# Spectra of neighbouring blocks: combined on VectorE, or accumulated in PSUM

## The chip, the cores and the metric

The kernel runs on one core of one Trainium2 chip. The metric is the device time of one execution in microseconds, the median of several runs. Every run that is quoted here was in the fast state, and each experiment was timed against the kernel before, in the same rounds and on the same chip. The experiments ran in four sets, each on a chip of its own, so a comparison of two of them from different sets is good to some tenths of a us only (the median of the kernel before was 357.57 to 358.05 us in these sets). A verdict of faster or slower needs 2%, which is 7.2 us here; what is discussed below is mostly smaller than that, so the intervals matter more than the verdicts.

## The reference

Two layers, each an H3-style block (a 4-tap shift convolution on `k`, a product with `v`, a long causal convolution by FFT, a product with `q`) and a SwiGLU feed-forward block. `k`, `v` and all weights are the same in both layers.

```python
def _A_ref(q, k, v, shift_k, ssm_k, ssm_D):          # S = 2048, D = 512, 4 taps
    k_shift = 0
    for t in range(ks):
        k_shift = k_shift + k_pad[:, t:t + S, :] * shift_k[:, ks - 1 - t]
    kv = k_shift * v
    y = irfft(rfft(kv, padded) * rfft(ssm_k, padded))[:S]    # causal convolution per channel
    y = y + kv * ssm_D
    return q * y

def _B_ref(x, w_gate, w_up, w_down):                  # F = 1792
    return (silu(x @ w_gate) * (x @ w_up)) @ w_down

for _ in range(2):
    x = x + _A_ref(layernorm(x), A_k, A_v, A_shift_k, A_ssm_k, A_ssm_D)
    x = x + _B_ref(layernorm(x), B_w_gate, B_w_up, B_w_down)
```

All tensors are bf16.

## The kernel before

The long convolution is cut into 4 blocks of 512 rows. A block `b` of the long kernel `h` gets a spectrum `H[b]` by matmuls with cosine and sine tables (`fwd`), copied out of PSUM (the memory that TensorE's matmuls write to; this copy is called evacuation) by ScalarE and finished by additions and subtractions of its parts (butterflies) on VectorE. The spectrum that the products need, `G[b]`, belongs to an overlapped kernel: the h of block `b` together with the h of block `b-1`. Before, `G[b]` is put together on VectorE from two finished spectra:

```python
def by_residue(rows, ev, scale, ring, engs, conv):
    for r in range(R):                                   # R = 4 residues
        for part, f in enumerate(("C", "nS")):           # real, imaginary
            ps = new(ring, "ps", [P, D], F32)
            add("PE", pe(1), ... mm(ps.t[:], [(fT(f, r), rows.t[:, r, :])]) ...)
            evacuate(ps, ev, (2 * r + part,), ..., scale, engs[...], conv)

def fold_h(b):
    h, hp = butterfly4(H[b], True, first if b == 1 else ()), H[b - 1]
    g = G[b] = spectrum(f"G{b}")
    for part, op in ((0, ALU.subtract), (1, ALU.add)):
        dve(4 * D, ... nc.vector.tensor_tensor(out=g.t[:, :, part, :], in0=h.t[:, :, part, :],
                                               in1=hp.t[:, :, 1 - part, :], op=op), ...)
```

`add` does not issue an instruction. It puts an operation with a planned duration into a plan, which a list scheduler orders per engine; `due` dates, the stretch factors and the start times at the top of the file are constants that were found by a search. So any change of an operation or of a constant can reorder all engines, and planned durations (`lat` for a DMA) decide only the order, not the truth.

Three other parts matter below. The h of a block is turned either by TensorE (`transpose_h`) or by a ScalarE copy and DMA transposes on SyncE's queue (`transpose_h_dma`, for the blocks in `H_DMA`):

```python
def transpose_h_dma(b):
    for dt in range(KD):
        add("ACT", ..., nc.scalar.copy(out=hr.t[:, :, dt], in_=hn[b].t[:, dt, :].rearrange(...)))
    for r in range(R):
        turned[b] = add("SP", 1.25, ... nc.sync.dma_start_transpose(out=hs.t[:, r]..., in_=hr.t[:, r]) ...)
```

The shift convolution of a block runs either on TensorE (`shift_mul`: 64 matmuls of 128 columns with diagonal matrices `dg`, which VectorE builds from the taps) or, for the blocks in `K_ACT`, as 16 scaled copies on ScalarE, three sums on VectorE and DMA transposes (`shift_mul_t`). And the taps are loaded as four rows of 1 KB, first on SyncE's queue, and turned by four small TensorE transposes:

```python
tapR = new("dn", "tapR", [KD, P, KS])
add("SP", 0.5, lambda: nc.sync.dma_start(out=tapR.t[:],
    in_=A_shift_k.rearrange("(dt p) j -> dt p j", p=P)), w=[tapR], lat=2.4, due=-70)
...
def turn_taps():
    for j in range(KS):
        nc.tensor.transpose(pt4.t[:, j, :], tapR.t[:, :, j], ident.t[0:KD, 0:KD])
add("DVE", 0.1, lambda: nc.vector.tensor_copy(out=tapT.t[:], in_=pt4.t[:].rearrange("p j dt -> p dt j")), ...)
for dt in range(KD):
    add("DVE", 0.6, ... tensor_tensor(out=dg.t[:, dt], ident (broadcast), tapT.t[:, dt, :] (broadcast), mult))
```

In the names of the profile, `kTb`, `vt` and `hs` are k, v and h of a block in the layout that the next step needs (`hn` and `hr` are h before it is turned), `dg` the diagonal matrices, `G` and `H` the spectra, `z` and `ptz` the normalised rows and their transposes for the feed-forward block, and `pf`, `sg` and `ht` its gate and up products. `wm` are dummy matmuls, which only keep TensorE at work until data are there.

## Time and profile before

| | before |
|---|---|
| median of 2 runs | 357.74 us (357.62 to 357.85) |
| span of the profiled execution (which took 358.32 us) | 356.5 us |
| TensorE (PE) busy | 347.6 us, 97% |
| VectorE (DVE) busy | 281.1 us, 79% |
| ScalarE (ACT) busy | 238.0 us, 67% |
| start of the first spectrum on TensorE | 14.34 us |

The busy line, the slices, the waits and the groups of before are shown in the prediction below. What it does not show is the start, instruction by instruction. In the timeline the columns are the start in us, the duration, the engine, the line and the operation, what it writes and reads, the shape and the number of instructions; in brackets, if any, the idle time before and what ended it.

```profile
5.63 2.50 DVE L933 TENSOR_TENSOR dg<-ident,tapT 128x512 bf16<-128x512 bf16 x4
7.07 1.05 PE L379 MATMUL pt<-ident,kn 128*128 128x128 bf16 x16
8.05 2.44 DVE L385 COPY kTb<-pt 128x512 bf16<-128x512 bf16 x2
10.77 3.74 PE L335 MATMUL ps<-dg,kTb 128*128 128x128 bf16 x64
14.34 3.62 PE L335 MATMUL ps<-hs,fwd 128*128 128x512 bf16 x15
```

VectorE builds the four diagonal matrices first and has finished just as TensorE's first transposes of k come in, so its two copies of k follow at once. The 64 shift matmuls start at 10.77 us and the first spectrum at 14.34.

### The profile page before, as it was taken

To read this page: it belongs to the slowest core of one execution; us is meant where nothing else is said; L and a number is where in the kernel's file an instruction comes from. 1 tells how busy PE (TensorE), PEld (TensorE's weight loads), DVE (VectorE), ACT (ScalarE), POOL (GpSimd) and SP (SyncE) were. 2 spreads that over 40 slices of the span, in tenths; PEclk is the share of its full clock that TensorE was granted. 3 is DMA by queue.
4 is the path that set the end of the run, shared out by engine and by line. 5 is a ranking of instruction groups with operands and counts; after the bars stand their busy time and mean duration, and the time that the engine had idled before them with its cause. 6 is when DMAs were issued, how large, how long until landed. Compare 5 with 4: busy or idle time off the path is not lost.

```text
span 356.5 us, 6735 instructions
## 1 busy us (share of the span) xinstructions
PE 347.6 (97%) x2689; PEld 254.4 (71%) x2712; DVE 281.1 (79%) x517; ACT 238.0 (67%) x454; POOL 39.3 (11%) x42
## 2 busy tenths in 40 slices
PE   7999999999999999999999999999999999999996
PEld 6655985867778585868668685858686777768673
DVE  6997999999989999999999999889985323626020
ACT  4587693838878493648878994848484775647352
POOL 1010010130320200111121000201101000101000
PEclk9999999999999999999999999999999999999999
DMA  7999021010241341010311042010103020101000
GB/s 263 306 353 293 2 69 22 0 31 2 45 119 45 63 147 31 0 31 1 79 40 31 1 116 63 2 29 3 31 29 31 30 31 1 31 1 31 30 2 29
DMA packets 37897, 21.98 MB, mean 62 GB/s; under 512 B 29797, under 2 KB 35690, under 8 KB 37866
## 3 DMA queue, kind: packets, MB, share of 16 engines
q1 hardware_dynamic: 37336, 21.03, 22.9%
q10 hardware_dynamic: 530, 0.53, 0.5%
q8 instruction: 21, 0.34, 0.4%
q14 instruction: 10, 0.08, 0.1%
HBM read 12.33 MB, written 2.10 MB: 40 GB/s over the span
## 4 chain that ended last, share of the span: by engine, by line
PE 49%; DVE 35%; ACT 10%; POOL 3%; issue 2%; DMA 1%; ACTq 0%; POOLq 0%; DVEq 0%
PE pf L335 30%; PE pd L851 15%; DVE m L518 4%; DVE ht L844 3%; DVE bnst L706 3%; DVE t L641 3%; DVE t L635 3%; DVE t L651 2%; POOL rstd L736 2%; ACT H L423 2%; DVE Z L656 2%; PE ps L335 2%; PE wm L1020 1%; DVE t L620 1%; DVE Z L648 1%
## 5 line engine op out<-in xcount | busy, mean ns | idle before, releaser
L335 PE MATMUL pf<-zT,wu_sb 128*128 128x256 bf16 x896 | 116.1, 273 | 0.1
L335 PE MATMUL pf<-zT,wg_sb 128*128 128x256 bf16 x896 | 116.1, 273 | 0.0
L335 PEld LDWEIGHTS <-wg_sb 128*128 128x128 bf16 x896 | 87.6, 98 | 18.9 <-issue 0.8
L851 PE MATMUL pd<-wd_sb,ht 128*128 128x512 bf16 x434 | 98.6, 380 | 1.5 <-DVE ht L844 0.8
L335 PEld LDWEIGHTS <-wu_sb 128*128 128x128 bf16 x896 | 87.6, 98 | 11.1
L837 ACT ACTIVATE sg<-pf 128x512 bf16<-128x512 f32 x112 | 68.9, 615 | 18.2 <-PE pf L335 16.7
L851 PEld LDWEIGHTS <-ht 128*128 128x128 bf16 x448 | 43.6, 98 | 49.8 <-DVE ht L844 1.2
L841 ACT CAST ht<-pf 128x512 bf16<-128x512 f32 x112 | 67.3, 601 | 15.0 <-PE pf L335 14.6
L844 DVE TENSOR_TENSOR ht<-ht,sg 128x1024 bf16<-128x1024 bf16 x64 | 39.5, 619 | 25.7 <-ACT ht L841 25.7
L711 POOL TENSOR_TENSOR rstd<-ve,nhalf 128x2 f32<-128x2 f32 x25 | 26.0, 1039 | 203.2 <-DVE ve L709 180.8
L706 DVE BATCH_NORM_STATS2 bnst<-xc 128x6 f32<-128x512 bf16 x50 | 32.5, 685 | 6.2 <-ACT xc L857 5.6
L863 ACT CAST dn<-pd 128x512 bf16<-128x512 f32 x24 | 12.9, 591 | 34.5 <-PE pd L851 34.5
L870 DVE TENSOR_TENSOR xc<-xc,dn 128x1024 bf16<-128x1024 bf16 x12 | 8.2, 686 | 17.8 <-ACT dn L863 17.8
L635 DVE TENSOR_TENSOR t<-X,G 128x2048 bf16<-128x2048 bf16 x18 | 21.9, 1219 | 0.0
L641 DVE TENSOR_TENSOR t<-X,G 128x2048 bf16<-128x2048 bf16 x18 | 21.9, 1217 | 0.0
L736 POOL TENSOR_TENSOR rstd<-ve,nhalf 128x2 f32<-128x2 f32 x7 | 12.0, 1719 | 80.0 <-DVE ve L732 80.0
L423 ACT ACTIVATE X<-ps 128x512 bf16<-128x512 f32 x32 | 18.8, 635 | 1.2 <-PE ps L335 1.1
L423 ACT ACTIVATE H<-ps 128x512 bf16<-128x512 f32 x24 | 13.4, 645 | 4.3 <-PE ps L335 4.3
L656 DVE TENSOR_TENSOR Z<-Z,t 128x2048 bf16<-128x2048 bf16 x12 | 14.7, 1222 | 0.1
L651 DVE TENSOR_TENSOR t<-t,t 128x2048 bf16<-128x2048 bf16 x12 | 14.6, 1221 | 0.1
L335 PE MATMUL ps<-vt,fwd 128*128 128x512 bf16 x54 | 14.4, 380 | 0.1
L335 PEld LDWEIGHTS <-fwd 128*128 128x128 bf16 x96 | 9.3, 98 | 7.2
(95 smaller groups left out, 316.5 us busy)
## 6 DMA issues: line engine op xcount, KB each, us to landing
vt<-in_A_v_dram SPq DMA_DIRECT2D x4, 512.0 KB, 4.6
xc<-in_A_q_dram SPq DMA_DIRECT2D x4, 512.0 KB, 4.8
out_dram<-xc SPq DMA_DIRECT2D x16, 128.0 KB, 1.7
wg_sb<-in_B_w_gate_dram SPq DMA_DIRECT2D x1, 1792.0 KB, 9.2
wu_sb<-in_B_w_up_dram SPq DMA_DIRECT2D x1, 1792.0 KB
wd_sb<-in_B_w_down_dram SPq DMA_DIRECT2D x1, 1792.0 KB, 12.3
hn<-in_A_ssm_k_dram SPq DMA_DIRECT2D x3, 512.0 KB, 7.6
hn<-in_A_ssm_k_dram ACTq DMA_DIRECT2D x1, 512.0 KB, 3.9
```

What stands on the lines that cost most here:

```text
L335: nc.tensor.matmul(o, lhsT=lhsT, rhs=rhs, start=(n == 0), stop=(n == len(terms) - 1))
L423: add("ACT", act(D), lambda: nc.scalar.activation(out=view(), in_=ps.t[:], func=ACT.Copy, scale=scale), r=[ps], w=[(buf, keys)], conv=conv)
L635: dve(n * D, lambda t1=t1, part=part: nc.vector.tensor_mul(out=t1.t[:], in0=x.t[:, sl, 0, :], in1=g.t[:, sl, part, :]), [(x, key(slots, (0 ...
L641: dve(n * D, lambda t2=t2, part=part: nc.vector.tensor_mul(out=t2.t[:], in0=x.t[:, sl, 1, :], in1=g.t[:, sl, 1 - part, :]), [(x, key(slots ...
L651: dve(n * D, lambda t1=t1, t2=t2, comb=comb: nc.vector.tensor_tensor(out=t1.t[:], in0=t1.t[:], in1=t2.t[:], op=comb), [t2], [t1], conv=conv)
L656: dve(n * D, lambda t1=t1, part=part: nc.vector.tensor_add(out=z.t[:, sl, part, :], in0=z.t[:, sl, part, :], in1=t1.t[:]), [t1], [zk], con ...
L706: add("DVE", 0.6, lambda st=st, i=i: nc.vector.bn_stats(out=st.t[:], in_=xs[c].t[:, i, :]), r=[(xs[c], (i,))], w=[st])
L711: add("POOL", PW, lambda: nc.gpsimd.tensor_tensor(out=rstd.t[:], in0=ve.t[:], in1=nhalf.t[:].to_broadcast((P, n)), op=ALU.pow), r=[ve, nha ...
L837: add("ACT", act(D), lambda ps=ps, o=o, sg=sg: nc.scalar.activation(out=sg.t[:, o:o + 2, :], in_=ps.t[:], func=ACT.Silu), r=[ps], w=[(sg, ...
L841: add("ACT", act(D), lambda ps=ps, o=o, ht=ht: nc.scalar.copy(out=ht.t[:, o:o + 2, :], in_=ps.t[:]), r=[ps], w=[(ht, (o // 2,))], due=(uni ...
L844: dve(n * W, lambda sg=sg, ht=ht: nc.vector.tensor_mul(out=ht.t[:], in0=ht.t[:], in1=sg.t[:]), [sg], [ht], due=(unit, k / pairs, 0.0, "h"))
L851: nc.tensor.matmul(pds[o].t[:], lhsT=ht.t[:, q, o * P:(o + 1) * P], rhs=wt["d"].t[:, ft, :], start=(ft == 0 and not xpe), stop=(ft == NF - 1))
```

## The change

The intent: a spectrum is linear, so `G[b]` can be accumulated in PSUM from the turned h of both blocks, with two matmuls in a tile instead of one. The two-input operations of `fold_h` go, six of 2048 elements in the program. To take TensorE work away in return, and to use VectorE's freed time, the shift convolution of block 2 moves off TensorE (`K_ACT`), and the transposes of block 1's h too (`H_DMA`). All searched constants are new. Two edits stand beside this: the taps are now loaded in their final layout by one DMA on ScalarE's queue, and a gate on the loads for block 2 is gone.

```diff
-H_DMA = lambda b: b in {2, 3}
+H_DMA = lambda b: b in {1, 2, 3}
-K_ACT = lambda b: b in {3}
+K_ACT = lambda b: b in {2, 3}
-RINGS = {}
+G_PE = True
+RINGS = {"hs": 2, "s8": 9} if G_PE else {}
 ... (SLK, ST1, ST2, ASL, HSL, Z_ACT, N_ACT, X_PE, T0, FLOOR, DUR, STRETCH: new values)
-          ("nC", 1, 3), ... ("S", 3, 0)]
+          ("nC", 1, 3), ... ("S", 3, 0), ("S", 0, 0)]
 ... (planned landings of the first loads: h 5.0 to 6.0, k 4.0 to 5.3, v 5.0 to 6.0, x 6.0 to 7.0)
     def spectrum_h(b, ring="pc"):
         hs = transpose_h_dma(b) if H_DMA(b) else transpose_h(b, ring, (0, 2), True)
-        H[b] = forward4(hs, "H", 2.0 / N, ring, True)
+        hss[b] = hs
+        H[b] = spectrum_g(b, ring) if G_PE else forward4(hs, "H", 2.0 / N, ring, True)
+
+    def spectrum_g(b, ring="pc"):
+        hs, hp = hss[b], hss[b - 1]
+        ev = spectrum(f"G{b}")
+        for r in range(R):
+            for part, fs in enumerate((("C", "S"), ("nS", "C"))):
+                ps = new(ring, "ps", [P, D], F32)
+                add("PE", pe(2), ... mm(ps.t[:], [(fT(f, r), t.t[:, r, :]) for f, t in zip(fs, (hs, hp))]), ...)
+                evacuate(ps, ev, (2 * r + part,), ..., 2.0 / N, "ACT", True)
+        return ev
     def fold_h(b):
+        if G_PE:
+            G[b] = butterfly4(H[b], True, first if b == 1 else ())
+            return
 ...
-    tapR = new("dn", "tapR", [KD, P, KS])
-    add("SP", 0.5, lambda: nc.sync.dma_start(out=tapR.t[:], in_=A_shift_k.rearrange("(dt p) j -> dt p j", p=P)), w=[tapR],
-        lat=2.4, due=-70)
+    add("ACT", 0.5, lambda: nc.scalar.dma_start(out=tapT.t[:], in_=A_shift_k.rearrange("(dt p) j -> p dt j", p=P)), w=[tapT],
+        lat=4.2, due=-60)
     load_h(0, "ACT", -59)
 ... (turn_taps and the copy behind it: removed)
         if c + 1 < NB:
-            gate = list(first) if c == 1 else ()
-            load_h(c + 1, after=gate)
-            load_k(c + 1, after=gate)
-            load_v(c + 1, after=gate)
+            load_h(c + 1)
+            load_k(c + 1)
+            load_v(c + 1)
```

More of the change, by code (lines that the diff above doesn't have):

```diff
@@ L19 @@
 NB = 4
-SLK = 8.52
-H_DMA = lambda b: b in {2, 3}
-ST1 = lambda l, c, h: (l, c, h) in {(0, 1, 1), (0, 2, 0), (0, 3, 0), (1, 0, 1)}
-ST2 = lambda l, c, h: (l, c, h) in {(0, 1, 1), (0, 3, 1), (1, 0, 0)}
-ASL = 8.04
-K_ACT = lambda b: b in {3}
+SLK = 10.9
+H_DMA = lambda b: b in {1, 2, 3}
+ST1 = lambda l, c, h: (l, c, h) in {(0, 0, 1), (0, 1, 0), (0, 2, 0)}
+ST2 = lambda l, c, h: (l, c, h) in {(0, 2, 0), (1, 1, 0), (1, 3, 0)}
+ASL = -36.31
+K_ACT = lambda b: b in {2, 3}
 PASSES = 1
@@ L28 @@
 PD_ACT, KV_ACT, ST_ACT = True, True, False
-HSL = 13.4
-Z_ACT = lambda l, c, h: (l, c, h) in {(0, 3, 1), (1, 1, 0), (1, 1, 1)}
-N_ACT = lambda l, c, h: (l, c, h) in {(0, 2, 0), (0, 2, 1), (1, 2, 1), (1, 3, 0), (1, 3, 1)}
+HSL = 21.03
+Z_ACT = lambda l, c, h: (l, c, h) in {(0, 0, 1), (0, 2, 0), (0, 2, 1), (0, 3, 0), (1, 0, 1), (1, 1, 0), (1, 1, 1), (1, 3, 1)}
+N_ACT = lambda l, c, h: (l, c, h) in {(0, 3, 1), (1, 0, 1), (1, 1, 1), (1, 2, 1), (1, 3, 1)}
 Z_DMA = lambda i, j: False
 D_DMA = lambda l, c, h: False
-X_PE = lambda l, c, h: (l, c, h) in {(0, 3, 1), (1, 1, 0), (1, 2, 0), (1, 3, 1)}
-RINGS = {}
-T0, FLOOR = 37.71, 9.21
-DUR = [20.73, 19.38, 17.95, 16.46, 26.14, 17.1, 26.09, 16.75, 22.3, 20.61, 21.16, 19.35, 17.53, 22.2, 16.85, 27.0]
-STRETCH = {1: {"PE": 2.88, "DVE": 1.23, "ACT": 4.33, "POOL": 1.0, "SP": 160.46},
-           2: {"PE": 3.08, "DVE": 1.77, "ACT": 1.75, "POOL": 1.0, "SP": 1.07},
-           3: {"PE": 3.04, "DVE": 1.08, "ACT": 2.72, "POOL": 1.0, "SP": 1.04}}
+X_PE = lambda l, c, h: (l, c, h) in {(0, 2, 0), (0, 2, 1), (0, 3, 1), (1, 0, 1), (1, 3, 1)}
+G_PE = True
+RINGS = {"hs": 2, "s8": 9} if G_PE else {}
+T0, FLOOR = 48.08, 19.94
+DUR = [16.0, 23.9, 26.05, 22.97, 21.86, 19.8, 19.06, 26.96, 19.52, 23.55, 21.07, 24.15, 16.63, 23.57, 17.87, 26.61]
+STRETCH = {1: {"PE": 8.53, "DVE": 2.37, "ACT": 2.97, "POOL": 1.0, "SP": 14.17},
+           2: {"PE": 2.62, "DVE": 1.0, "ACT": 1.41, "POOL": 1.0, "SP": 2.29},
+           3: {"PE": 6.2, "DVE": 1.34, "ACT": 1.62, "POOL": 1.0, "SP": 2.04}}
 R = 4
@@ L47 @@
           ("nS", 0, 2), ("nS", 1, 2), ("nS", 2, 2), ("nS", 3, 2),
-          ("nC", 1, 3), ("nC", 2, 3), ("nC", 3, 3), ("S", 1, 0), ("S", 2, 0), ("S", 3, 0)]
+          ("nC", 1, 3), ("nC", 2, 3), ("nC", 3, 3), ("S", 1, 0), ("S", 2, 0), ("S", 3, 0), ("S", 0, 0)]
 BI = {(f, r): i for i, (f, r, _) in enumerate(BLOCKS)}
@@ L338 @@
     NT = len(BLOCKS)
-    NI = NT // 2
+    NI = 7
     warm1 = whole("warm", [P, 1], F32)
@@ L344 @@
     dg = whole("dg", [P, KD, KS, P], parts=KD)
-    fwd, inv = whole("fwd", [P, NT, P], parts=4), whole("inv", [P, NT, P], parts=2)
+    fwd, inv = whole("fwd", [P, NT, P], parts=5), whole("inv", [P, 2 * NI, P], parts=2)
     wt = {"g": whole("wg_sb", [P, KD, F]), "u": whole("wu_sb", [P, KD, F]), "d": whole("wd_sb", [P, NF, D])}
@@ L358, in load_h @@
         q = nc.sync if eng == "SP" else nc.scalar
-        return add(eng, 0.55, lambda: q.dma_start(out=hn[b].t[:], in_=h3[:, :, b * L:(b + 1) * L]), w=[hn[b]], lat=(5.0, 10.0)[b] if b < 2 else 6.0, due=due, after=after)
+        return add(eng, 0.55, lambda: q.dma_start(out=hn[b].t[:], in_=h3[:, :, b * L:(b + 1) * L]), w=[hn[b]], lat=(6.0, 10.0)[b] if b < 2 else 6.0, due=due, after=after)
     def load_k(b, due=None, after=()):
@@ L363, in load_k @@
             kn[b] = new("s8", "kn", [P, R, D])
-            add("SP", 0.55, lambda: nc.sync.dma_start(out=kn[b].t[:], in_=k_t[:, b]), w=[kn[b]], lat=4.0, due=due)
+            add("SP", 0.55, lambda: nc.sync.dma_start(out=kn[b].t[:], in_=k_t[:, b]), w=[kn[b]], lat=5.3, due=due)
             return
@@ L389, in load_v @@
         vt[b] = new("v", "vt", [P, R, D], parts=R)
-        return add("SP", 0.6, lambda: nc.sync.dma_start(out=vt[b].t[:], in_=v_t[:, b]), w=[vt[b]], lat=4.5 if b else 5.0, due=due, after=after)
+        return add("SP", 0.6, lambda: nc.sync.dma_start(out=vt[b].t[:], in_=v_t[:, b]), w=[vt[b]], lat=4.5 if b else 6.0, due=due, after=after)
     def load_x(c, due=None, after=()):
         xs[c] = new("x", "xc", [P, R, D], parts=R)
-        return add("SP", 0.7, lambda: nc.sync.dma_start(out=xs[c].t[:], in_=q_t[:, c]), w=[xs[c]], lat=4.5 if c else 6.0, due=due, after=after)
+        return add("SP", 0.7, lambda: nc.sync.dma_start(out=xs[c].t[:], in_=q_t[:, c]), w=[xs[c]], lat=4.5 if c else 7.0, due=due, after=after)
     def load_weights(which, due, after=()):
@@ L435, in half @@
                 add("PE", pe(2), lambda ps=ps, terms=terms: mm(ps.t[:], [(fT(f, r), rows.t[:, r, :]) for f, r in terms]),
-                    r=[(rows, [r for _, r in terms]), fwd], w=[ps], conv=conv)
+                    r=[(rows, [r for _, r in terms]), (fwd, range(4))], w=[ps], conv=conv)
                 evacuate(ps, ev, (2 * slot + part,), lambda slot=slot, part=part: ev.t[:, slot, part], scale,
@@ L460, in direct @@
                 add("PE", pe(4), lambda ps=ps, terms=terms: mm(ps.t[:], [(fT(f, r), rows.t[:, r, :]) for f, r in terms]),
-                    r=[rows, fwd], w=[ps])
+                    r=[rows, (fwd, range(4))], w=[ps])
                 evacuate(ps, dst, (2 * slot + part,), lambda slot=slot, part=part: dst.t[:, slot, part], 1.0, engs[part],
@@ L545, in butterfly4 @@
         return ev
+    hss = {}
     def spectrum_h(b, ring="pc"):
         hs = transpose_h_dma(b) if H_DMA(b) else transpose_h(b, ring, (0, 2), True)
-        H[b] = forward4(hs, "H", 2.0 / N, ring, True)
+        hss[b] = hs
[6 more added lines that the diff above has]
+                ps = new(ring, "ps", [P, D], F32)
+                add("PE", pe(2), lambda ps=ps, fs=fs, r=r: mm(ps.t[:], [(fT(f, r), t.t[:, r, :]) for f, t in zip(fs, (hs, hp))]),
+                    r=[(hs, (r,)), (hp, (r,)), fwd], w=[ps], conv=True, dest=ev)
+                evacuate(ps, ev, (2 * r + part,), lambda r=r, part=part: ev.t[:, r, part], 2.0 / N, "ACT", True)
+        return ev
     def fold_h(b):
+        if G_PE:
+            G[b] = butterfly4(H[b], True, first if b == 1 else ())
+            return
         h, hp = butterfly4(H[b], True, first if b == 1 else ()), H[b - 1]
@@ L922 @@
             r=[(fwd, (n,))], w=[(fwd, (part,))])
+    add("DVE", 0.14, lambda: nc.vector.tensor_scalar(out=fwd.t[:, NT - 1, :], in0=fwd.t[:, 4, :], scalar1=-1.0, scalar2=None,
+                                                     op0=ALU.mult), r=[(fwd, (1,))], w=[(fwd, (4,))], due=30.0)
     tapF = whole("tapF", [P, KD, KS], F32)
-    pt4 = new("pf", "pt4", [P, KS, KD], BF16)
-    def turn_taps():
-        for j in range(KS):
-            nc.tensor.transpose(pt4.t[:, j, :], tapR.t[:, :, j], ident.t[0:KD, 0:KD])
-    add("PE", 0.25, turn_taps, r=[tapR, ident], w=[pt4])
-    add("DVE", 0.1, lambda: nc.vector.tensor_copy(out=tapT.t[:], in_=pt4.t[:].rearrange("p j dt -> p dt j")), r=[pt4], w=[tapT])
     add("DVE", 0.1, lambda: nc.vector.tensor_copy(out=tapF.t[:], in_=tapT.t[:]), r=[tapT], w=[tapF])
@@ L939 @@
     add("DVE", 0.34, lambda: nc.vector.tensor_add(out=hs.t[0:1, 0, :], in0=hs.t[0:1, 0, :], in1=drow.t[:]), r=[drow], w=[(hs, (0,))])
+    hss[0] = hs
     shift_mul(0, "pf", False)
@@ L953, in go @@
                 nc.tensor.transpose(it.t[:, i, :], fwd.t[:, n * NI + i, :], ident.t[:])
-        add("PE", pe(NI, P), go, r=[fwd, ident], w=[it])
+        add("PE", pe(NI, P), go, r=[(fwd, range(4)), ident], w=[it])
         add("ACT", act(NI * P), lambda it=it, n=n: nc.scalar.copy(out=inv.t[:, n * NI:(n + 1) * NI, :], in_=it.t[:]),
```

## The prediction

> **What bounds the kernel now.** I read the page first for the busy shares and the forty slices.
>
> ```profile
> PE 347.6 (97%) x2689; PEld 254.4 (71%) x2712; DVE 281.1 (79%) x517; ACT 238.0 (67%) x454; POOL 39.3 (11%) x42
> ...
> PE   7999999999999999999999999999999999999996
> ...
> DVE  6997999999989999999999999889985323626020
> ```
>
> The reader is to see TensorE without a gap between the second and the last slice, and VectorE nearly full for about 30 of the 40 slices but never alone. A busy TensorE need not run at its peak, so I went next to the chain that ended last, in order of time, where nothing but feed-forward matmuls stand after 190 us:
>
> ```profile
> 310.18 6.04 PE pd L851 x28
> 316.22 12.23 PE pf L335 x112
> ```
>
> That is 6.04/28 = 0.216 us for a 512-column matmul and 12.23/112 = 0.109 us for a 256-column one, back to back. For 128 columns the timeline has 64 of them in 3.74 us, of which some 0.16 us is the drain of the last, so about 0.056 us each. With these rates I counted the recorded matmuls of each 20 us window: 20.1 us of matmul work in 40 to 60, 19.6 in 60 to 80, 20.0, 20.2, 20.1 and 20.0 in the next four, 19.6 in 160 to 180, 19.8, 19.8, and 20.0 on average after that. So TensorE is not only busy, it is at its rate from 20 us to the end; the slack in all those windows together is under 2 us. What is left idle or cold is the start (8.4 of the first 20 us) and the end (3.7 us after the last full stretch). Third view, who waited for whom on TensorE:
>
> ```profile
> PE wm L1020 <- POOL ident masks.py:199: 1.7, 1, 1.7
> PE pt L475 <- ACT kTb L383: 1.5, 2, 0.8
> PE pd L851 <- DVE ht L844: 0.8, 2, 0.6
> ```
>
> These are all its named waits. Only the last, 0.8 us, is VectorE's doing. Hence the time is start + TensorE work + under 2 us of stalls + tail. VectorE appears with 35% in the chain of waits because its convolution backlog reaches 190 us, but TensorE fills that time with other units.
>
> **What the Trainium skill says.** "TensorE: Matmul & The Clock Gate", section Back-to-back issue gap, gives N/2.4 + 2.5 ns warm, thus 215.7 and 109.2 ns for 512 and 256 columns: the two chain lines above agree to the last digit. (Its other figure there, 131 ns sustained for 512 columns, does not fit this trace.) "PSUM — Partial Sum Buffer", section The four PSUM rules: a matmul without the first flag adds to what its group has written. So the sum of two neighbouring blocks costs one more matmul and no more evacuations; the 32 X0 spectra of this kernel, four terms each, already work so. "VectorE: DVE Perf Modes", section The perf-mode tier table, has 1224 ns for a bf16 two-input operation of 2048 elements; the trace has 1215 and 1218 for the very instructions that go. The first of these pages, section Part 1: The HAM clock gate, says that the clock is halved until some 3.4 to 4 us of matmuls have run; here the dummy matmuls start 0.107 us apart and speed up only after about 6.2 us.
>
> **The change part by part.** The order of instructions per engine gives exact counts; TensorE first, since it is the bound. The groups touched:
>
> ```profile
> L335 PE MATMUL ps<-dg,kTb 128*128 128x128 bf16 x192 | 11.7, 219 | 0.1
> L335 PE MATMUL ps<-hs,fwd 128*128 128x512 bf16 x39 | 11.7, 379 | 0.2
> ...
> L475 PE MATMUL pt<-ident,hn 128*128 128x128 bf16 x32 | 2.5, 219 | 1.5 <-ACT kTb L383 1.5
> ```
>
> - Two-term spectra of h: 24 evacuated tiles now take two matmuls each (40 to 64 in the program): 24 x 0.216 = +5.2 us.
> - The shift convolution of block 2 goes from TensorE to ScalarE and DMA transposes: 192 to 128, 64 x 0.056 = -3.6 us.
> - The transposes of h for block 1 go to ScalarE and DMA: 32 to 16, 16 x 0.056 = -0.9 us.
> - One more unit adds its residual by an identity matmul (8 to 10): +0.4 us.
> Sum on the bound: **+1.1 us**. The dummy matmuls (46 to 64) are no work but fill the start.
>
> VectorE: the combination goes,
>
> ```profile
> L555 DVE TENSOR_TENSOR G<-H 128x2048 bf16<-128x2048 bf16 x4 | 4.8, 1215 | 0.0
> ...
> L555 DVE TENSOR_TENSOR G<-H,G 128x2048 bf16<-128x2048 bf16 x2 | 2.4, 1218 | 0.0
> ```
>
> -7.2 us. The moved shift adds three 2048-element sums, 3.6 us. Ten normalisations of 0.41 us move to ScalarE, -4.1, with five small scale tiles back, +0.8; two more pairs of row statistics, +1.7; one residual sum less, -0.7. Net about **-6 us**, beside TensorE work: the wait it could remove is the 0.8 us above. ScalarE: 16 scaled copies of k at 0.8 us, ten normalisations at 0.8, four copies of h at 0.7, minus the statistics, four ks and two hs copies: about **+15 us** of 238, also beside.
>
> The start is on the path. The taps now come by one DMA of 8-byte pieces behind the first h, where before four 1 KB rows came first and TensorE turned them. k is issued about 0.46 us earlier, but the rewritten program plans later landings for all first loads and puts 64 dummies in one run. Before, 46 dummies and the taps ended at 7.03 us and k's transposes began at 7.07. 64 from 1.72 us, cold at 0.107 until about 6.2 and then 0.06, end near 7.5 to 7.7: **+0.5 us**.
> Then the first unit's own chain. ScalarE gets four h copies and one statistics pass among the eight X0 evacuations; stepping through its order with the trace's durations, the last evacuation is 2.3 us later and the last Z some 1.6 us later. TensorE has its 16 transposes no longer as filler there, so it idles about **+0.7 us** before the last inverse matmuls. Behind them 14 inverse and 16 spectrum matmuls (6.5 us) cover the 6 us until the normalised rows are back, provided that the DMA transposes of h, queued behind the weights, keep up.
> Elsewhere I take **-1.0 us**, my choice: all tuned constants were searched anew, and a lighter VectorE should close part of the under 2 us of scattered stalls and of the wait for ht. Sum: +1.1 + 0.5 + 0.7 - 1.0 = +1.3, so 357.7 becomes 359.0 us.
>
> **The rivals.** (a) VectorE's relief is worth more than TensorE's extra, so it gets faster by several us. For it: VectorE is mostly at 95% and more until 260 us and holds 35% of the chain. Against: TensorE at its rate in those windows leaves under 2 us to win; even with all of it and nothing lost at the start, 357.7 + 1.1 - 2 = 356.8. (b) ScalarE becomes a local bound. For it: summing durations unit by unit in the new order, one unit of block 1 has 22.2 us of TensorE, 21.7 of VectorE and 20.9 of ScalarE, a later one 21.7, 21.6 and 21.5, so any misfit there is paid; 2 to 3 us, thus 361 to 362. Against: before too had units where VectorE's sum was above TensorE's (22.2 against 20.2), and other units took it up. (c) The start: taps or h transposes land late behind the weight loads (the page shows 353 GB/s in that slice), and VectorE or TensorE waits; 1 to 3 us more, up to 362. (d) The extra matmuls are hidden in idle TensorE: the windows speak against it.
>
> **Range and chances.** The lower end 356.8 is (a) at its fullest; the upper 361.5 is the sum with half of (b) or (c). 2% is 7.2 us, and neither the work counted nor any rival reaches it: faster 0.02, same 0.96, slower 0.02.
>
> **What would show it.** In the changed profile, TensorE's busy share should stay at 97%, the spectrum group should show 64 matmuls and the shift group 128, and the 20 us windows should again hold 19.5 to 20 us of work. VectorE should fall to about 275 us busy and ScalarE rise to about 253. k's transposes should begin at about 7.6 us, and TensorE show a new wait for Z near 30 us. I am wrong if TensorE's windows show more than 2 us of new gaps between 60 and 200 us (then b), if the first feed-forward matmul comes over 3 us later (then c), or if TensorE's gaps before vanish and the start is not later (then a).

## The result and the profile after

The changed kernel takes 362.74 us (median of 2 runs, 362.55 to 362.92) against 357.74, a ratio of 1.014 with a 95% interval of 1.0096 to 1.0183. The changed kernel run again, in other rounds, gave 362.24 and 1.0134 [1.0108, 1.016], with 361.35 to 363.44 in four runs. Ratios here are the mean time of one kernel's fast runs over that of the other's of the same rounds, so not quite the ratio of the medians. The change makes the kernel about 5.0 us slower; that is within 2%, as expected, but above the predicted range, whose upper end was 361.5.

The page of the changed kernel, busy shares and two of the slices:

```profile
PE 350.8 (97%) x2646; PEld 254.5 (70%) x2672; DVE 275.6 (76%) x508; ACT 252.4 (70%) x470; POOL 34.6 (10%) x42
...
PE   7699999999999999999999999999999999999996
...
DVE  3888789999999994699999999999995423525120
```

TensorE is full from the third slice on, as before. Its second slice fell from 9 to 6, VectorE's first from 6 to 3. The loss is at the left edge. TensorE's named waits (in all, how often, the longest):

```profile
PE wm L1033 <- POOL ident masks.py:199: 1.7, 1, 1.7
PE pt L476 <- ACT kTb L384: 1.5, 2, 0.8
PE pt L476 <- DVE kTb L386: 1.1, 1, 1.1
PE ps L336 <- DVE kTb L386: 0.5, 1, 0.5
PE pf L336 <- ACT sg L856: 0.4, 1, 0.4
```

Two of the new ones, 1.6 us, are on VectorE's copies of k. The timeline of the start shows why these are late and what follows:

```profile
1.23 0.52 ACTq L909 DMA_DIRECT2D tapT<-in_A_shift_k_dram  x1
...
7.56 1.05 PE L380 MATMUL pt<-ident,kn 128*128 128x128 bf16 x16
...
8.83 1.90 DVE L946 TENSOR_TENSOR dg<-ident,tapT 128x512 bf16<-128x512 bf16 x3 [3.48 <-DMA tapT<-in_A_shift_k_dram]
...
10.64 2.43 DVE L386 COPY kTb<-pt 128x512 bf16<-128x512 bf16 x2
...
13.13 5.21 PE L336 MATMUL ps<-dg,kTb 128*128 128x128 bf16 x64 [0.55 <-DVE kTb L386]
```

VectorE idles 3.48 us for the taps. Its first copy of k is behind three `dg` operations in its order, so it comes at 10.64 us instead of 8.05, and the shift matmuls start at 13.13 instead of 10.77. Then the same 64 matmuls take 5.21 us instead of 3.74. The windows say why; after the width, the columns are busy time and count of TensorE, weight loads, VectorE, ScalarE and GpSimd, then the granted TensorE clock, the DMA share and GB/s. After:

```profile
7.50:13.13 5.63, 2.43 (x33) 2.00 (x32) 4.30 (x6) 3.46 (x4) 0.00 (x0) 0.98 1.04 396
13.13:18.18 5.05, 5.05 (x64) 5.05 (x64) 4.12 (x9) 1.45 (x4) 0.00 (x0) 0.69 1.13 220
```

Before:

```profile
7.50:13.13 5.63, 4.15 (x71) 3.89 (x69) 5.32 (x10) 3.45 (x4) 0.00 (x0) 1.00 0.95 338
10.77:14.34 3.57, 3.57 (x67) 3.57 (x66) 3.22 (x9) 0.46 (x1) 0.00 (x0) 1.00 1.13 393
```

After a stretch in which TensorE worked 2.43 of 5.63 us, the clock was granted at 0.69 on average while the shift matmuls ran; before, with 4.15 us of work in the same stretch, it stayed at 1.00. The Trainium skill describes this in "TensorE: Matmul & The Clock Gate", section Part 1: The HAM clock gate: half the clock after an idle window of about 3.4 us. The trace agrees on the halved rate (matmuls of this group start 0.107 us apart until about 16 us), though TensorE was never idle for 3.4 us at a stretch here. But from the first dummies to the next matmuls that are no transposes it ran only transposes. This stretch was 5.41 to 6.05 us long in the four profiles in which the clock fell at the start (the changed kernel's two, a_gate and b_newtaps), and 4.42 us at most in the fourteen others, in which it did not. Whether transposes count as work for the clock was not tested.

The first spectrum thus starts at 18.18 us, 3.84 later than before. The chain that ended last, in order of time (start, duration, what), tells the same story:

```profile
1.23 7.50 DMA tapT<-in_A_shift_k_dram
8.83 1.90 DVE dg L946 x3
10.72 2.36 DVE kTb L386 x2
13.13 5.43 PE ps L336 x65
```

From the first spectrum to the end the profiled span has 361.1 - 18.18 = 342.9 us, against 356.5 - 14.34 = 342.2 before. That difference, 0.8 us, is near the +1.1 of counted matmul work (the profiled execution of before was 0.6 us above its median, so the difference may be larger). The groups, with count, busy time and mean ns:

```profile
L336 PE MATMUL ps<-hs,fwd 128*128 128x512 bf16 x58 | 15.9, 379 | 0.3
...
L336 PE MATMUL ps<-dg,kTb 128*128 128x128 bf16 x128 | 9.2, 240 | 0.5 <-DVE kTb L386 0.5
...
L476 PE MATMUL pt<-ident,hn 128*128 128x128 bf16 x16 | 1.4, 218 | 2.6 <-ACT kTb L384 1.5 <-DVE kTb L386 1.1
```

They are as predicted: 128 shift matmuls and 16 transposes of h, and 58 of the 64 spectrum matmuls are recorded. On this reading, the explanation was simple: the new way of loading the taps costs 3.8 us, and the rest behaves. The experiments show that it is not that simple.

### The profile page after: what moved, and what is told of

Same layout as the page of the kernel before. It is cut to its first block, busy times and chain, and to the rows that moved or that the text cites. A ratio compares the mean times of both kernels' runs of the same rounds, so it can differ in the third digit from the quotient of the medians.

```text
span 361.1 us, 6673 instructions
## 1 busy us (share of the span) xinstructions
PE 350.8 (97%) x2646; PEld 254.5 (70%) x2672; DVE 275.6 (76%) x508; ACT 252.4 (70%) x470; POOL 34.6 (10%) x42
## 3 DMA queue, kind: packets, MB, share of 16 engines
q10 hardware_dynamic: 1058, 0.53, 0.5%
## 4 chain that ended last, share of the span: by engine, by line
PE 73%; DVE 11%; ACT 10%; DMA 2%; issue 1%; ACTq 0%; POOL 0%; POOLq 0%; DVEq 0%
PE pf L336 41%; PE pd L870 21%; PE ps L336 9%; DMA tapT<-in_A_shift_k_dram 2%; DVE m L519 2%; PE ps L713 2%; ACT G L424 2%; ACT sg L856 2%; ACT ka L597 1%; DVE ht L863 1%; ACT ht L860 1%; DVE bnst L725 1%; ACT kc L597 1%; DVE X L525 1%; DVE Z L675 1%
## 5 line engine op out<-in xcount | busy, mean ns | idle before, releaser
L730 POOL TENSOR_TENSOR rstd<-ve,nhalf 128x2 f32<-128x2 f32 x26 | 27.3, 1051 | 236.7 <-DVE ve L728 171.3
L725 DVE BATCH_NORM_STATS2 bnst<-xc 128x6 f32<-128x512 bf16 x52 | 33.6, 684 | 4.0 <-ACT xc L876 3.5
L882 ACT CAST dn<-pd 128x512 bf16<-128x512 f32 x22 | 11.8, 592 | 28.8 <-PE pd L870 28.8
L336 PEld LDWEIGHTS <-fwd 128*128 128x128 bf16 x120 | 11.6, 98 | 9.6 <-DMA hs<-hr 0.4
L876 ACT CAST xc<-pd 128x512 bf16<-128x512 f32 x10 | 5.4, 590 | 16.9 <-PE pd L870 16.9
L336 PE MATMUL ps<-hs,fwd 128*128 128x512 bf16 x58 | 15.9, 379 | 0.3
L795 DVE TENSOR_TENSOR n<-n,Yk 128x1024 bf16<-128x1024 bf16 x15 | 10.3, 690 | 6.6 <-ACT Yk L699 5.6
```

What stands on the lines that cost most here:

```text
L336: nc.tensor.matmul(o, lhsT=lhsT, rhs=rhs, start=(n == 0), stop=(n == len(terms) - 1))
L725: add("DVE", 0.6, lambda st=st, i=i: nc.vector.bn_stats(out=st.t[:], in_=xs[c].t[:, i, :]), r=[(xs[c], (i,))], w=[st])
L730: add("POOL", PW, lambda: nc.gpsimd.tensor_tensor(out=rstd.t[:], in0=ve.t[:], in1=nhalf.t[:].to_broadcast((P, n)), op=ALU.pow), r=[ve, nha ...
```

## The experiments

### Is it the taps' load?

**a_oldtaps** is the changed kernel with the old load of the taps.

```diff
-    add("ACT", 0.5, lambda: nc.scalar.dma_start(out=tapT.t[:], in_=A_shift_k.rearrange("(dt p) j -> p dt j", p=P)), ...)
+    tapR = new("dn", "tapR", [KD, P, KS])
+    add("SP", 0.5, lambda: nc.sync.dma_start(out=tapR.t[:], in_=A_shift_k.rearrange("(dt p) j -> dt p j", p=P)), ..., due=-70)
 ... (turn_taps and its copy as before)
```

> The changed kernel with only the load of the taps put back: four rows of 1 KB issued first, turned on TensorE. Theory (the late taps are what the prediction missed): taps are on VectorE by about 5.6 us, the shift matmuls of block 0 start near 11.2 us and the first spectrum matmul near 14.8 us instead of 18.2, so 362.7 - 3.4 = about 359.3 us. Rival (the spectra, the moved shift or the shifted schedule cost it; the taps are hidden): at least 361.5 us.

Measured: 363.22 us, 1.0152 [1.0135, 1.0169]. The theory as stated fell: nothing was won, though the first spectrum now starts at 15.07 us, 3.1 earlier than in the changed kernel. A new wait has swallowed it, the first line of TensorE's waits:

```profile
PE ps L336 <- DMA hs<-hr: 2.7, 1, 2.7
```

The timeline of this kernel shows the wait and its origin on SyncE's queue (SPq lines are issues, with the time that the queue was held by them):

```profile
22.85 8.90 SPq L368 DMA_TRANSPOSE kTb<-in_A_k_dram  x1
...
27.36 0.81 ACT L584 COPY hr<-hn 128x512 bf16<-128x512 bf16 x1
31.85 5.20 SPq L588 DMA_TRANSPOSE hs<-hr  x4
...
35.15 1.04 PE L336 MATMUL ps<-hs,fwd 128*128 128x512 bf16 x4 [2.73 <-DMA hs<-hr]
```

ScalarE has h of block 1 ready for the DMA transposes at 28.17 us, but SyncE is held by the transposing load of block 2's k until 31.75 and issues them only then. The transposes of the first feed-forward input (`ptz`) come at 39.85 us; in the changed kernel they came at 39.81. In the changed kernel this second path was there too, hidden: its h copies ended at 31.29, and its transposes were issued at 31.31.

```profile
21.11 7.97 SPq L368 DMA_TRANSPOSE kTb<-in_A_k_dram  x1
...
30.49 0.80 ACT L584 COPY hr<-hn 128x512 bf16<-128x512 bf16 x1
31.31 5.28 SPq L588 DMA_TRANSPOSE hs<-hr  x4
```

The kernel before has neither: its gate puts block 2's loads of h and k later in SyncE's order (k's is issued at 27.08 us), and TensorE turns the h of block 1.

**b_newtaps** is the converse: the kernel before with only the new load of the taps.

```diff
-    tapR = new("dn", "tapR", [KD, P, KS]) ... (and turn_taps)
+    add("ACT", 0.5, lambda: nc.scalar.dma_start(out=tapT.t[:], in_=A_shift_k.rearrange("(dt p) j -> p dt j", p=P)), ..., due=-60)
```

> The kernel before with only the new load of the taps (8-byte pieces, second on ScalarE's queue). Theory: the taps land at 8.5 to 9 us again, the first spectrum matmul comes 3 to 4 us later than 14.3, and the time is 361 to 361.5 us. Rival (taps are hidden): 357.7 to 358.3 us.

Measured: 360.94 us, 1.008 [1.0053, 1.0106], with 359.81 to 362.42 in five runs. The first spectrum starts at 17.90 us. So the load alone costs about 2.9 us where no second path hides it: the cause is sufficient in the old kernel.

**a_planlate** leaves the load and tells the planner that it lands late, which puts 29 dummy matmuls into the gap and, on VectorE, the copies of k ahead of the `dg` operations.

```diff
-        lat=4.2, due=-60)
+        lat=7.0, due=-60)
```

> The changed kernel, where only the planner is told that the taps land late (7 us instead of 4.2): it then puts 29 dummy matmuls in the gap ahead of the shift matmuls and the copies of k ahead of the taps' diagonal on VectorE. The data still land at 8.8 us. Theory (of the 3.8 us lost at the start 1.5 us are a halved TensorE clock after the idle gap): the 64 shift matmuls take 3.6 to 3.8 us instead of 5.2 at a granted clock of 1.0, and the time falls by about 1.5 us to 361.2. Rival (the clock does not matter, only the data's arrival does): 362.5 or more.

Measured: 362.57 us, 1.013 [1.0115, 1.0145], so -0.2. The clock did what was hoped for:

```profile
10.18 1.78 PE L1033 MATMUL wm<-ident 128*128 128x128 bf16 x29
11.80 3.87 PE L336 MATMUL ps<-dg,kTb 128*128 128x128 bf16 x64
15.51 1.46 PE L336 MATMUL ps<-hs,fwd 128*128 128x512 bf16 x6
```

The shift matmuls take 3.87 us again, and the first spectrum is 2.7 us earlier than in the changed kernel. It is lost again: a wait of 1.3 us for `hs<-hr` appears and the time stays. (The first 64 dummies took 5.03 us here and 5.78 in the changed kernel, so two profiles of the same start differ by up to some 0.7 us by when the clock is granted.)

**a_tapsfirst** keeps the load in small pieces but issues it first, on SyncE's queue, to tell "small pieces" from "behind h".

```diff
-    add("ACT", 0.5, lambda: nc.scalar.dma_start(out=tapT.t[:], ...), lat=4.2, due=-60)
+    add("SP", 0.5, lambda: nc.sync.dma_start(out=tapT.t[:], ...), lat=4.2, due=-200)
```

> The changed kernel with the same 8-byte load of the taps, but issued first of all on the SyncE queue. Theory 1 (the taps are late because their 512 small pieces wait behind the 512 KB of h on the same queue): they land by about 4 to 5 us, the first spectrum comes near 15 us and the time is about 359.5 us. Theory 2 (512 pieces of 8 bytes are slow in themselves wherever they stand): they land at 7 us or later, or hold up k behind them by as much, and the time stays at 361.5 to 363.

Measured: 363.33 us, 1.0158 [1.0141, 1.0176]. The load now lands 3.3 us after its issue instead of 7.5:

```profile
tapT<-in_A_shift_k_dram SPq DMA_DIRECT2D x1, 4.0 KB, 3.3
```

The `dg` operations begin at 4.80 us, with the taps there in time, and the first spectrum starts at 15.18. So the pieces of 8 bytes alone did not make the taps late; their place behind the 512 KB of h is needed too. The run changed the queue and the order together, so it does not tell a place on that queue from being issued later. Whether larger pieces in that same place would have been in time was not tried. The Trainium skill warns of both in "DMA: Bandwidth & Descriptors": section Rules for kernel authors ("Many small transfers": coalesce) and section Queues, rings and completion order (on each DMA engine descriptors are taken in ring order). These two landings fit the second; on the first, ScalarE's queue went from 530 packets to 1058, 528 more for 4 KB. The time again won nothing, with a wait of 3.1 us for `hs<-hr`.

### Is it two paths that hide each other?

The new theory: in the changed kernel two chains reach `ptz` at nearly the same time, the late taps and the DMA transposes of h behind block 2's loads. To undo one gives nothing, to undo both gives about 3 us. **a_gate** undoes the second alone.

```diff
+            gate = list(first) if c == 1 else ()
-            load_h(c + 1)
-            load_k(c + 1)
-            load_v(c + 1)
+            load_h(c + 1, after=gate)
+            load_k(c + 1, after=gate)
+            load_v(c + 1, after=gate)
```

> The changed kernel with only the old order of the loads of block 2 on the SyncE queue: h transposes of block 1 ahead of the 8 to 9 us long transposing load of k for block 2. Theory (two paths meet at the row transposes before the first feed-forward matmul: late taps on one, the SyncE queue on the other, and either alone holds the same moment): TensorE has no wait for h left, but its own stream from the late first spectrum still ends at 39.4 to 39.8, so no more than 0.5 us is won: 362.3 to 362.9. Rival (the SyncE queue alone is the loss): about 359.5 us.

Measured: 362.54 us, 1.0119 [1.01, 1.0138]. The first spectrum starts at 18.16 and `ptz` at 39.67 us, against 18.18 and 39.81: nothing won, as expected. **a_oldtaps_gate** undoes both (the two edits above together).

> Both parts undone: taps by rows and the old order of the loads on SyncE. Theory (two paths): the transposes of h are issued from about 28.2 us instead of 31.9, the row transposes come near 36.6 us instead of 39.9, and the time is 360.0 us (359.3 to 360.5), the matmul count alone being +1.1 on 357.7 and k's transposes starting 1 us later. Rival (something after the start, such as the fuller ScalarE, costs the rest): above 361.5 us.

Measured: 359.70 us, 1.0059 [1.0036, 1.0081]. So 3.0 us come back when both are undone (2.8 against a_gate of the same rounds) and none when either is. The timeline:

```profile
27.16 0.83 ACT L584 COPY hr<-hn 128x512 bf16<-128x512 bf16 x1
28.02 5.31 SPq L588 DMA_TRANSPOSE hs<-hr  x4
```

The transposes are issued as soon as the copies are done. The first spectrum starts at 14.88 and `ptz` at 36.38 us, 3.4 earlier than in the changed kernel.

**a_gate_planlate** (gate restored, and `lat=7.0`) splits the 3 us further: late taps, but no cold clock and no second path.

> The changed kernel with the old load order on SyncE, taps still late, but 29 dummy matmuls planned into the gap ahead of the shift matmuls. Now that the SyncE path is out of the way, theory (a halved clock is part of the taps' cost): the shift matmuls take 3.9 us instead of 5.2 and the time falls from 362.5 to about 361 us; the rest down to 359.7 is the taps' own lateness. Rival (the clock costs nothing here either): 362 us or more.

Measured: 361.63 us, 1.0103 [1.0086, 1.012]. Against a_gate that is -0.9, which would be the cold clock's part, and the 1.9 us from there to 359.70 the lateness of the taps itself, as `dg` can then no longer be built before k is there. This split is not shown: the edit changes VectorE's order too, the two runs are of different sets and their intervals overlap, and this profile had its first transposes of k at 7.86 us and that of a_planlate at 6.81, the scatter named above.

| version | first spectrum, us | `ptz`, us | median, us |
|---|---|---|---|
| changed kernel | 18.18 | 39.81 | 362.74 |
| old taps alone | 15.07 | 39.85 | 363.22 |
| gate alone | 18.16 | 39.67 | 362.54 |
| both | 14.88 | 36.38 | 359.70 |

Against the kernel before of their own rounds these are +5.0, +5.2, +4.8 and +2.0 us. From `ptz` to the end the four profiled spans have 321.3 to 321.6 us each, so what the two repairs win lies ahead of `ptz`. The second profile of the changed kernel (after3, below) shows the second path directly: its first spectrum comes at 17.62 us, yet `ptz` at 40.36, with a wait of 1.0 us for `hs<-hr`.

### Where does the mended version stand, and what is VectorE's relief worth?

The version with both undone, called mended below, is still 2.0 us slower than before. Its PSUM accumulation takes 7.2 us off VectorE. Is that relief free of value, because TensorE is the bound? **a_oldtaps_gate_nog** switches it off in the mended version and leaves all other constants (the buffer rings, `RINGS`, go back with it).

```diff
-G_PE = True
+G_PE = False
```

> As the run with taps and load order undone, but with the spectra of the overlapped kernels combined on VectorE again, all other constants of the changed kernel kept: 24 matmuls of 512 columns less, six 2048-element VectorE operations more. Theory (TensorE is the bound at its rate): 5.2 us less than that run, about 354.8 us, faster than the kernel before. Rival (with the shift of block 2 moved too, VectorE becomes the bound without the spectra's relief): 358 us or more, with TensorE waits for VectorE between 60 and 260 us.

Measured: 375.19 us, 1.0473 [1.0451, 1.0495], correct. The expectation fell by 20 us. TensorE's waits begin with:

```profile
PE pf L336 <- DMA zT<-z: 6.4, 1, 6.4
PE pd L870 <- DVE ht L863: 6.1, 5, 2.1
```

VectorE has 282.7 us of work, 6.8 more than the mended version, and TensorE waits for it, directly (`ht`) and through the normalised rows that it makes (`z`). But the planner reordered everything with constants that were searched for other work, so the size says little. The same holds for the next two. **b_g** is the kernel before with the PSUM accumulation alone:

```diff
+G_PE = True
-RINGS = {}
+RINGS = {"hs": 2, "s8": 9}
 ... (spectrum_g, fold_h, the block ("S", 0, 0) as in the change)
```

> The kernel before with only the spectra accumulated in PSUM (and the buffer rings it needs); taps, load order, shifts and all constants as before. Theory (TensorE bound): +24 x 0.216 = +5.2 us, 362.9 us. Rival (VectorE's 7.2 us of relief pays for it): 357 to 359 us.

Measured: 366.52 us, 1.0238 [1.0223, 1.0254]. Of the 8.8 us, 5.2 are the counted matmuls, if they are paid in full; the other 3.6 would be gaps of the new order, such as 18.0 us of TensorE work in the 20 us from 80 on. **b_kact** is the kernel before with block 2's shift moved off TensorE, without the relief:

```diff
-K_ACT = lambda b: b in {3}
+K_ACT = lambda b: b in {2, 3}
```

> The kernel before with only block 2's shift convolution moved to ScalarE and DMA transposes, all other constants as before. Theory (TensorE bound): -64 x 0.056 = -3.6 us, 354.1 us, faster than both kernels. Rival (VectorE, which gets 3.3 us more, and ScalarE, 10 us more, are too tight in the middle of the kernel): 357 us or more, with TensorE waiting for ht or zT.

Measured: 369.34 us, 1.0335 [1.0307, 1.0364], where a gain was expected. The first waits of TensorE:

```profile
PE pf L335 <- DMA zT<-z: 5.9, 3, 3.4
PE pf L335 <- ACT sg L837: 2.7, 2, 2.4
```

To settle the worth of each engine's time without the planner in the way, the next five runs keep every engine's order and change only the work. **b_pe24** issues the 24 spectrum matmuls of h twice in the kernel before, with the scale halved, so the result is the same.

```diff
-   mm(ps.t[:], [(fT(f, r), rows.t[:, r, :])])
+   mm(ps.t[:], [(fT(f, r), rows.t[:, r, :])] * twice)     # twice = 2 for H, 1 else; scale / twice
```

> The kernel before with each of the 24 one-term matmuls of h's spectra issued twice into the same tile (scale halved, same result), the order of all else unchanged: the change's extra TensorE work alone. Theory (TensorE at its rate is the bound, every matmul is paid): +24 x 0.216 = +5.2 us, 362.9 us. Rival (they fit into idle TensorE time): 358 to 359 us.

Measured: 361.62 us, 1.0108 [1.0092, 1.0123]: +3.9 for 5.2 us of matmuls. **ag_dve** issues six VectorE operations of 2048 elements twice in the mended version, +7.3 us of VectorE.

```diff
-   nc.vector.tensor_tensor(out=dst.t[:, lo:lo + 2], in0=src.t[:, 0:2], in1=src.t[:, 2:4], op=op)
+   for _ in range(2 if src.name.startswith("G") else 1): nc.vector.tensor_tensor(... as before ...)
```

> The changed kernel with taps and load order undone (359.7 us), in which the six 2048-element operations that open the butterflies of the combined spectra are issued twice (same result), the order of all else unchanged: VectorE gets back the 7.3 us that the change takes from it. Theory of the prediction (VectorE's relief lies beside TensorE's work and is worth at most 1 us): 359.7 to 361 us. Rival (in this schedule VectorE has become as tight as TensorE, and the relief is what pays): 363 to 367 us, with TensorE waiting for VectorE's ht in the second half of the convolutions.

Measured: 367.08 us, 1.0253 [1.0235, 1.0271], +7.4 us against the mended version's 359.70: in full. TensorE's waits begin with `ht` and with a ScalarE copy of the shift:

```profile
PE pd L871 <- DVE ht L864: 2.9, 3, 1.3
PE ps L336 <- ACT ks L499: 2.4, 1, 2.4
```

**b_dve6** does the same to the kernel before (with "H" for "G").

> The kernel before with its six 2048-element operations that open the butterflies of h issued twice (same result, the order unchanged): +7.3 us on VectorE. If VectorE was already as tight as TensorE before the change: +6 to +8 us, 364 to 366 us. If it had the slack that the prediction read: under +2 us, below 359.7 us.

Measured: 364.33 us, 1.019 [1.0174, 1.0205], +6.8 us for 7.3. So VectorE had no slack there either, although TensorE's waits of before name it for 0.8 us only. **b_cheapcomb** takes VectorE work away: the kernel before with each combination made a plain copy, 3.2 us less (not the whole 7.2). It computes a wrong spectrum on purpose (the convolution's share in the output is small enough that the comparison did not object).

```diff
-   nc.vector.tensor_tensor(out=g.t[:, :, part, :], in0=h.t[:, :, part, :], in1=hp.t[:, :, 1 - part, :], op=op)
+   nc.vector.tensor_copy(out=g.t[:, :, part, :], in_=h.t[:, :, part, :])
```

> Wrong results on purpose: the kernel before, in which the six combining operations on VectorE (1.22 us each) are copies of the same size (about 0.7 us each), the order unchanged: 3.2 us of VectorE relief without any TensorE work. If the relief by itself pays: 354.5 us. If TensorE's own rate stands in the way, as the prediction had it (under 2 us to win): 356.5 to 357.7 us.

Measured: 357.36 us, 0.9996 [0.9987, 1.0005], so -0.2 us, nothing. **ag_pe24less** takes TensorE work away: the mended version without the second matmul of the 24 tiles, wrong on purpose too.

```diff
-   mm(ps.t[:], [(fT(f, r), t.t[:, r, :]) for f, t in zip(fs, (hs, hp))])
+   mm(ps.t[:], [(fT(f, r), t.t[:, r, :]) for f, t in zip(fs, (hs, hp))][:1])
```

> Wrong results on purpose: the changed kernel with taps and load order undone (359.7 us), in which the second matmul of each of the 24 accumulated spectra is left out, the order of all else unchanged. If TensorE is the bound there throughout: -24 x 0.216 = -5.2 us, 354.5 us. If VectorE is the tighter one, as the run with 7.3 us more on VectorE suggests: 358 us or more. If both are equally tight, something between, about 356.5 us.

Measured: 358.03 us, 1.0017 [1.001, 1.0023]: only -1.7 against the mended version for 5.2 us less work. TensorE's waits there, after the start, name ScalarE (`G`, `sg`, `Yk`: 2.0 us) and `hs<-hr` (0.8), not VectorE. **after3**, the changed kernel again in the same rounds, was there to show that these rounds agree with the first ones.

> The changed kernel itself once more, timed in rounds against the kernel before on one chip: 362.7 us, ratio 1.014.

Measured: 362.24 us, 1.0134 [1.0108, 1.016].

| edit, order kept | work on the engine, us | time, us |
|---|---|---|
| before, TensorE more | +5.2 | +3.9 |
| before, VectorE more | +7.3 | +6.8 |
| before, VectorE less | -3.2 | -0.2 |
| mended, VectorE more | +7.3 | +7.4 |
| mended, TensorE less | -5.2 | -1.7 |

In the kernel before, more work on either engine is paid for the most part, and less on VectorE alone gives nothing. In the mended version more of VectorE's work is paid in full, and less of TensorE's gives a third. That fits a VectorE which is the tighter of the two there, but more TensorE work and less VectorE work were not tried on it. The VectorE work was added at one place only, the butterflies of the spectra, so the two rows speak of that stage. The mended rows compare runs of different sets.

## Why the prediction was right or wrong

**The counts** were right: the groups of 64, 128 and 16, TensorE's share of 97%, VectorE's 275.6 us (about 275 predicted), ScalarE's 252.4 (about 253). The transposes of k at 7.56 us (about 7.6) were in part luck: in the second profile of the same kernel they came at 7.05, because the 64 dummies took 5.27 us there and not 5.78. (The 6.2 us that the prediction gives for the speed-up of the dummies count from the start of the span, 4.5 us after the first of them.) The windows between 60 and 200 us hold 19.8 to 20.0 us of busy TensorE each, so its rival (b), ScalarE as a local bound, did not come. That the class is "within 2%" was right as well.

**The start was the step that failed.** The prediction had it at "+0.5 us", from the end of the dummies to k's transposes. That half microsecond was there (7.07 to 7.56), but this was not the path: `dg` waits for the taps, copies of k stand behind `dg` in VectorE's order, and the shift matmuls stand behind both. The old start shows it too: in the five other profiles that have it (b_cheapcomb, b_dve6, b_pe24, b_g, b_kact) k's transposes begin anywhere from 6.43 to 7.30 us, and the first spectrum stays at 14.35 to 14.46. The prediction mentioned the 8-byte pieces and their place behind h and gave them no landing time. Measured, this is +3.84 us at the first spectrum, of which 1.5 are the slower shift matmuls at a granted clock of 0.69. In execution time, start and queue together are worth the 3.0 us between the changed kernel and the mended one.

**The second path** was named by the prediction as a condition ("provided that the DMA transposes of h, queued behind the weights, keep up") and in rival (c), "taps or h transposes land late", at 1 to 3 us more. That rival is what happened, with both halves of it at once, and each hides the other; what held the queue was not the weights but block 2's transposing load of k. The prediction let only half of this rival into its range, and half of 1 to 3 us on its 359.0 gives 360.5 at most, not the 361.5 that it states; 362.74 is above even the 362 of the whole rival. The sign for (c), a first feed-forward matmul over 3 us later, appeared: 37.09 to 44.04 us. Not all of this is delay, as the new order puts all 64 shift matmuls of block 1 ahead of it, and the mended version has 40.70; the 3.3 us between these two are.

**The waits at the first unit, "+0.7 us"**, did not appear: neither the changed kernel nor the mended one has a named wait for Z near 30 us.

**The gain elsewhere, "-1.0 us"**, did not come. After the start, TensorE's named waits before were 0.8 us (`ht`); in the mended version they are 0.7 us (0.5 for `sg`, 0.2 for `ht`). The reason behind it was that VectorE's net -6 us lies "beside TensorE work". That holds in one direction only. The part of the relief that was tried by itself (3.2 us) gave no gain, as the prediction had it and against rival (a). But added VectorE work was paid nearly in full, so VectorE had no room to spare. It may be that the relief is what the moved shift needs: without it that move cost 11.6 us, but in an order that the search had not been run for, so this is not shown.

**The sum, put right.** Of the 5.0 us, 3.0 are the taps and the queue together (mended against changed, in runs), and 2.0 remain. They fit +1.1 of counted matmul work and +0.5 of start (14.34 to 14.88 us), with 0.4 us that no run places and that lie within the interval (1.0036 to 1.0081, thus some 0.8 us either way). This is a fit and no experiment: added matmuls cost 3.9 us for 5.2 in the kernel before, and taken away from the mended version they gave 1.7.

**What stays open.** What the 2.0 us of the mended version are made of; how much of the losses of the three re-planned versions (a_oldtaps_gate_nog, b_g, b_kact) is the work and how much the unsuited order; and whether a new search of the constants on the mended version would bring it under 357.74. No version that was run is shown to be better than the kernel before.

## What to carry to other kernels

Follow every new load to the first instruction that uses it, in that engine's order, and count what stands behind it; a 4 KB load can hold the whole start. When a repair frees a wait and the time doesn't move, look for the wait that took its place and undo both together before you give the cause up. In a kernel where two engines are both full, test each with more and with less work at an unchanged order: the named waits alone called VectorE harmless here, and more work on it was not.

## What the Trainium skill lacked or had wrong

- "TensorE: Matmul & The Clock Gate" gives sustained rates of about 131 ns for a 512-column and 81 ns for a 128-column matmul in a stream of weight loads and matmuls. The traces show 216 ns (28 in 6.04 us) and, for 128 columns, 64 in the 3.57 us from 10.77 to 14.34, thus 56 ns. Its formula, N/2.4 + 2.5 ns, which it calls that of the isolated matmul, is the one that fits here, and other parts of the page have such rates for back-to-back matmuls too.
- The same page ties the halved clock to an idle window of about 3.4 us and does not say how little work makes a window idle. Here the granted clock was 0.69 in a stage after 5.63 us in which TensorE was busy for 2.43 us, nearly all of it transposes, with no single pause over 1.11 us; with 4.15 us of work in the same stretch it stayed at 1.00. As no run tests whether transposes count, this does not show the page wrong.
- "DMA: Bandwidth & Descriptors" states no time to landing for a small load in many pieces behind a large one on the same queue. 4 KB in 512 pieces landed 7.5 us after the issue behind a load of 512 KB, and 3.3 us after it when issued first.
- The same page gives a bandwidth for DMA transposes, but not how long one such load holds the queue that issues it while other loads are in flight. The same load (528 x 512 bf16 from HBM) held it for 7.55 to 10.71 us for block 1, 4.63 to 9.22 for block 2 and 1.94 to 2.90 for block 3 in these runs. In a_oldtaps the transposes of h, ready at 28.17 us, were issued behind it at 31.85.
